# A decode-attention kernel re-cut into key quarters of all 16 heads, with its K turned on VectorE and one softmax for all

## Chip, cores, metric

One core of one Trainium2 chip. The metric is the device time of one execution in microseconds (us). A time is the median of several runs, or one run where that is said; the span of the profiled execution is some 2 us shorter than its run's time. Each run on record carries a state: "slow" when it is over 1.5% above the fastest of its kernel, "unknown" when it is single.

## The reference, cut to what matters

One decode step for a batch of 2: a layer norm of `x`, an attention over a sliding window of a K and V cache, and a gate from a small ReLU network. All inputs are bfloat16.

```python
# B, D = 2, 448;  Hq, Hkv, Sk, Dh = 16, 8, 8192, 256;  W = 2048 (the last 2048 keys)
q = (xn @ wq).reshape(B, 1, Hq, Dh)                    # wq: 448 x 4096
k, v = k_cache[:, :, Sk - W:], v_cache[:, :, Sk - W:]  # [2, 8, 2048, 256], two q heads share one
o = softmax(q k^T / 16) v
s = o.reshape(B, 1, 4096) @ wo                         # wo: 4096 x 448
g = silu(relu(xn @ w1) @ w2)                           # w1: 448 x 1792, w2: 1792 x 448
out = x + s * g
```

What must be read is 44.1 MB: 16.8 MB of K, 16.8 MB of V, and 10.5 MB of weights. "16 heads" below means the 2 x 8 pairs of batch and KV head. In the caches, the same key of two neighbouring heads lies 8192 x 256 x 2 bytes = 4 MiB apart.

## The kernel before

K and V come in four units of 4 MiB. A unit is four heads of one batch with all 2048 keys. Each SBUF partition gets one piece of 32 KiB (64 keys). The order of the source is "row of 64 keys outside, head inside":

```python
def kv_src(u, cache):
    b, v = divmod(u, 2)
    return cache[b, 4 * v:4 * v + 4, SK - W:SK, :].rearrange("h (r t) d -> r h (t d)", t=NT)  # NT = 64
# as built: source [step 32 KiB, 32] [step 4 MiB, 4] [32 KiB] -> 128 partitions of 32 KiB
```

PE (TensorE, the matrix engine) turns each K piece (as fp32 pairs of bf16), and VectorE (DVE) and ScalarE (ACT) evict it, that is, copy it out of PSUM:

```python
o = pr.op(PE, lambda e, n=n, lo=lo: e.matmul(bank_f[:, n * 128:(n + 1) * 128],
    lhsT=src_f[:, lo:lo + 128], rhs=ident_f[:, :], start=True, stop=True, is_transpose=True), deps)
...                                                     # cut
if i not in ON_ACT:
    evac[n_th] = pr.op(DVE, lambda e: e.tensor_copy(dst[:, :], bank[:, :]), deps)
else:
    evac[n_th] = pr.op(ACTE, lambda e: e.activation(dst[:, :], bank[:, :], ACT.Copy), deps)
```

Every unit has its own softmax chain (maximum, transposed maximum, shift, exp, transposed weights), and PV (weights times V) of a unit runs beside the scores of the next. The tail multiplies the attention output with `wo`, 32 row blocks of four matmuls each, none column-tiled, while the last pieces of `wo` land. All loads go through one queue, issued by SyncE (SP) in program order.

## Time and profile before

| | before |
|---|---|
| time, median of the first 3 runs | 112.46 us (112.26 to 113.44) |
| span of the profiled run | 110.4 us |
| read from HBM | 44.11 MB |
| PE, DVE, ACT busy | 71%, 45%, 33% of the span |

From the page of the profile of the kernel before: busy time and share of the span by engine, then the rate of the DMA in 40 equal slices of the span.

```profile
span 110.4 us, 1966 instructions
PE 78.2 (71%) x862; PEld 54.9 (50%) x867; DVE 49.4 (45%) x114; ACT 35.9 (33%) x44; POOL 2.3 (2%) x12
...
DMA  3989989998999899999999999999999999999930
GB/s 63 508 380 451 499 356 423 491 439 380 433 487 404 380 411 416 406 495 415 478 427 386 427 487 404 398 451 451 404 415 463 395 436 412 387 418 414 395 134 1
```

The same as a table of stretches. The columns are: the stretch in us, its length, the busy time (and instructions) of each engine, the granted clock of PE (1.00 is full), the DMA share (mean busy share of the 16 engines) and the rate.

```profile
core 0: us, PE busy (x) PEld busy (x) DVE busy (x) ACT busy (x) POOL busy (x), PEclk, DMA share, GB/s
20.00:30.00 10.00, 8.69 (x100) 6.54 (x103) 5.85 (x12) 4.99 (x6) 0.00 (x0) 1.00 1.02 438
...
40.00:50.00 10.00, 8.26 (x87) 5.08 (x87) 5.68 (x13) 3.88 (x5) 0.00 (x0) 1.00 1.03 430
...
80.00:90.00 10.00, 10.00 (x90) 8.12 (x88) 5.96 (x10) 6.77 (x7) 0.00 (x0) 0.88 0.98 418
...
105.00:107.00 2.00, 1.92 (x40) 1.75 (x38) 0.00 (x0) 0.00 (x0) 0.00 (x0) 1.00 0.43 167
```

The DMA share is near 1 from 2 to 105 us at about 425 GB/s, so the loads bound this kernel. No engine is busy all the time.

The groups of work that the change removes:

```profile
L301 PE MATMUL tb<-ident_f,kbuf 128*128 128x128 f32 x256 | 35.7, 300 | 10.9 <-DMA kbuf<-in_A_k_cache_dram 10.9
...
L311 ACT ACTIVATE kt<-tb 128x1024 bf16<-128x1024 bf16 x28 | 27.4, 1023 | 27.0 <-PE tb L301 27.0
L309 DVE COPY kt<-tb 128x1024 bf16<-128x1024 bf16 x36 | 24.7, 689 | 23.5 <-PE tb L301 23.4
```

The end of the chain of work that ended last (start us, length us, what):

```profile
79.70 27.09 DMA kbuf<-in_A_wo_dram
106.79 0.04 issue
106.83 1.36 PE obk L281 x24
...
108.22 0.27 DVE tmp L556
...
108.51 0.26 DVE out_sb L558
```

`wo` comes in six pieces. The one that lands at 106.79 us is the fifth: it releases the last 24 matmuls, and 3.6 us of work and store follow. The sixth and last is issued at 80.17 us and lands at 107.35, while they run; from there to the end it takes 3.1 us. Its line in the list of transfers (size, us from issue to landing):

```profile
kbuf<-in_A_wo_dram SPq DMA_DIRECT2D x1, 224.0 KB, 27.2
```

### The profile page before, as it was taken

How to read it: one execution, taken by the hardware profiler on the slowest of the kernel's cores; microseconds unless marked ns; L12 is line 12 of the kernel's file. 1: busy time of each engine (PE TensorE's matmuls, PEld its weight loads, DVE VectorE, ACT ScalarE, POOL GpSimd, SP SyncE). 2: the span in 40 equal slices, each digit the busy share in tenths (PEclk: the TensorE clock that was granted, in tenths of full speed). 3: DMA queues.
4: the chain of work that ended last, by engine and by line, in shares of the span. 5: the costliest groups of instructions: out<-in, count | busy, mean ns of one | idle time of the engine just before them, and what ended most of it. 6: DMA issues, size and time to landing. Idle time of an engine off the chain costs nothing.

```text
span 110.4 us, 1966 instructions
## 1 busy us (share of the span) xinstructions
PE 78.2 (71%) x862; PEld 54.9 (50%) x867; DVE 49.4 (45%) x114; ACT 35.9 (33%) x44; POOL 2.3 (2%) x12
## 2 busy tenths in 40 slices
PE   0010049997756999858589999856399985897991
PEld 0000049992322977322389876322397741335891
DVE  2292005485154666463401975463157655454001
ACT  4930004694002568402000948202046771200000
POOL 6200000000000000000000000000000000000000
PEclk9999999999999999999959999999859999999999
DMA  3989989998999899999999999999999999999930
GB/s 63 508 380 451 499 356 423 491 439 380 433 487 404 380 411 416 406 495 415 478 427 386 427 487 404 398 451 451 404 415 463 395 436 412 387 418 414 395 134 1
DMA packets 2907, 44.22 MB, mean 400 GB/s; under 512 B 338, under 2 KB 468, under 8 KB 1364
## 3 DMA queue, kind: packets, MB, share of 16 engines
q1 hardware_dynamic: 2864, 44.11, 94.2%
q8 instruction: 6, 0.10, 0.4%
q10 hardware_dynamic: 36, 0.01, 0.0%
q14 instruction: 1, 0.01, 0.0%
HBM read 44.11 MB, written 0.00 MB: 399 GB/s over the span
## 4 chain that ended last, share of the span: by engine, by line
PE 40%; DMA 37%; DVE 14%; SPq 3%; ACT 2%; issue 2%
DMA kbuf<-in_A_wo_dram 25%; PE tb L301 20%; DMA kbuf<-in_A_k_cache_dram 13%; PE sbk L281 6%; PE obk L281 4%; PE tb L281 4%; SPq L36 3%; DVE kt L309 2%; PE mbk L281 2%; DVE s_sb L351 2%; ACT e_sb L355 2%; DVE rm L334 2%; PE mbk L360 1%; DVE mrow L342 1%; PE mbk L339 1%
## 5 line engine op out<-in xcount | busy, mean ns | idle before, releaser
L301 PE MATMUL tb<-ident_f,kbuf 128*128 128x128 f32 x256 | 35.7, 300 | 10.9 <-DMA kbuf<-in_A_k_cache_dram 10.9
L301 PEld LDWEIGHTS tb<-ident_f,kbuf 128*128 128x128 f32 x256 | 31.9, 156 | 15.3 <-DMA kbuf<-in_A_k_cache_dram 11.0
L311 ACT ACTIVATE kt<-tb 128x1024 bf16<-128x1024 bf16 x28 | 27.4, 1023 | 27.0 <-PE tb L301 27.0
L309 DVE COPY kt<-tb 128x1024 bf16<-128x1024 bf16 x36 | 24.7, 689 | 23.5 <-PE tb L301 23.4
L281 PE MATMUL sbk<-kt,qz 128*32 128x512 bf16 x128 | 11.1, 393 | 1.6 <-DVE kt L309 1.1
L355 ACT ACTIVATE e_sb<-s_sb 128x512 bf16<-128x512 f32 x4 | 2.5, 629 | 21.4 <-DVE s_sb L351 21.4
L281 PE MATMUL obk<-vbuf,pt 128*16 128x512 bf16 x96 | 7.4, 379 | 0.0
L281 PE MATMUL obk<-kbuf,at_z 128*8 128x112 bf16 x128 | 7.0, 213 | 0.5 <-DMA kbuf<-in_A_wo_dram 0.3
L281 PEld LDWEIGHTS obk<-kbuf,at_z 128*8 128x8 bf16 x128 | 6.3, 87 | 1.0 <-DMA kbuf<-in_A_wo_dram 0.9
L281 PEld LDWEIGHTS sbk<-kt,qz 128*32 128x32 bf16 x128 | 2.7, 94 | 5.5 <-DVE kt L309 2.1
L281 PE MATMUL mbk<-ident,xg 2*128 2x2 bf16 x7 | 0.3, 163 | 6.6 <-DVE xg L246 6.6
L281 PE MATMUL tb<-qz,ident 128*128 128x512 bf16 x15 | 4.6, 382 | 0.3 <-issue 0.3
L334 DVE TENSOR_REDUCE rm<-sbk 128x4 f32<-128x512 f32 x4 | 2.8, 691 | 4.3 <-PE sbk L281 4.3
L281 PE MATMUL tb<-wf,h_z 128*8 128x112 bf16 x56 | 4.2, 258 | 0.4 <-DVE h_z L460 0.4
L281 PEld LDWEIGHTS tb<-wf,h_z 128*8 128x8 bf16 x56 | 4.1, 109 | 0.5 <-issue 0.5
L365 DVE COPY pt<-mbk 128x512 bf16<-128x512 bf16 x4 | 1.7, 424 | 5.0 <-PE mbk L360 5.0
L281 PEld LDWEIGHTS mbk<-ident,xg 2*128 2x128 bf16 x7 | 0.3, 101 | 6.6 <-DVE xg L246 6.6
L474 ACT ACTIVATE ea<-tb 8x112 f32<-8x112 f32 x1 | 0.3, 254 | 9.0 <-PE tb L281 9.0
L281 PE MATMUL mbk<-one_f,mall 1*128 1x1 f32 x8 | 1.5, 256 | 2.3 <-DVE mall L346 2.3
L339 PE MATMUL mbk<-ident_f,rm 128*1 128x128 f32 x4 | 1.1, 270 | 2.9 <-DVE rm L337 2.9
L351 DVE SCALAR_TENSOR_TENSOR s_sb<-sbk,bias,low 128x512 f32<-128x512 f32 x4 | 3.0, 751 | 0.1
L281 PEld LDWEIGHTS obk<-vbuf,pt 128*16 128x16 bf16 x96 | 2.1, 87 | 1.9
(77 smaller groups left out, 46.6 us busy)
## 6 DMA issues: line engine op xcount, KB each, us to landing
kbuf<-in_A_k_cache_dram SPq DMA_DIRECT2D x4, 4096.0 KB, 31.8
vbuf<-in_A_v_cache_dram SPq DMA_DIRECT2D x3, 4096.0 KB, 39.1
wf<-in_B_w_dram SPq DMA_DIRECT2D x2, 1568.0 KB, 43.8
vbuf<-in_A_v_cache_dram SPq DMA_DIRECT2D x1, 3072.0 KB, 19.6
vbuf<-in_A_wq_dram SPq DMA_DIRECT2D x1, 2560.0 KB, 19.7
kbuf<-in_A_wo_dram SPq DMA_DIRECT2D x2, 896.0 KB, 23.9
vbuf<-in_A_wq_dram SPq DMA_DIRECT2D x1, 1024.0 KB, 4.9
vbuf<-in_A_v_cache_dram SPq DMA_DIRECT2D x1, 1024.0 KB, 21.5
```

The lines of the kernel that those rows point to most:

```text
L36: o = _Op(eng, lambda e: e.dma_start(dst, src), [d for d in deps if d is not None], True)
L281: return lambda e: e.matmul(out_ap, lhsT=lhsT, rhs=rhs, start=start, stop=stop, skip_group_check=True, **kw)
L301: o = pr.op(PE, lambda e, n=n, lo=lo: e.matmul(bank_f[:, n * 128:(n + 1) * 128], lhsT=src_f[:, lo:lo + 128], rhs=ident_f[:, :], start=True ...
L309: evac[n_th] = pr.op(DVE, lambda e: e.tensor_copy(dst[:, :], bank[:, :]), deps)
L311: evac[n_th] = pr.op(ACTE, lambda e: e.activation(dst[:, :], bank[:, :], ACT.Copy), deps)
L334: v = pr.op(DVE, lambda e: e.tensor_reduce(out=rm4[:, :], in_=view(sbk, 0, [[1, 4], [4, 128]]), axis=AX.X, op=ALU.max), [st["S", u]])
L339: m = st["rmT", u] = pr.op(PE, lambda e: e.matmul(mbk_ap(0, 128, 1), lhsT=rm[:, :], rhs=ident_f[:, :], start=True, stop=True, is_transpose ...
L342: v = pr.op(DVE, lambda e: e.tensor_reduce(out=mrow[0:1, :], in_=view(mbk, 0, [[1, 8], [8, 16]], n=1), axis=AX.X, op=ALU.max, negate=True) ...
L351: v = st["shift", u] = pr.op(DVE, lambda e: e.scalar_tensor_tensor(out=s_sb[:, :], in0=sbk[:, :], scalar=bias[:, 0:1], in1=low[:, :], op0= ...
L355: a = st["exp", u] = pr.op(ACTE, lambda e: e.activation(e_sb[:, :], s_sb[:, :], ACT.Exp, accum_out=ssum[:, 0:1]), [v, st.get(("Pt", u - 1) ...
L360: o = pr.op(PE, lambda e, j=j: e.matmul(mb16[:, 512 + 128 * j:640 + 128 * j], lhsT=e_sb[:, 128 * j:128 * j + 128], rhs=ident[:, :], start= ...
L365: v = st["pt", u] = pr.op(DVE, lambda e: e.tensor_copy(view(pt[u % 2], 0, [[256, 2], [16, 16], [8, 2], [1, 8]]), view(mb16, 512, [[256, 2] ...
```

## The change

The intent: take 256 PE transposes and 64 evictions out, do one softmax for everything instead of four, and shorten the tail by column tiling. A unit is now a quarter of the keys (512) of all 16 heads, so that every row of scores belongs to one head; all K comes first, then all V. The core of the diff (cut; the setup of masks and selectors is left out):

```diff
         def kv_src(u, cache):
-            b, v = divmod(u, 2)
-            return cache[b, 4 * v:4 * v + 4, SK - W:SK, :].rearrange("h (r t) d -> r h (t d)", t=NT)
+            lo = SK - W + u * NT * NR                                     # NR = 8
+            return cache[:, :, lo:lo + NT * NR, :].rearrange("b h (r t) d -> (b h) r (t d)", t=NT)
...
         def do_T(u, i):                                                   # now do_T(u, blk)
-            ... 4 PE transposes into a PSUM bank, then a copy on DVE or ACT
+            st["T", u] = st["kt", u, blk] = pr.op(DVE, lambda e: e.transpose(
+                view(dst, 32 * NT * blk, [[1, 32 * NT]]), view(src, 32 * blk, [[DH // 2, NT], [1, 32]])),
+                [d_k[u], st.get(("S", u - 1, blk))])
...
-        def softmax(u, fill=()):                                          # once per unit
+        st["bias"] = pr.op(DVE, ... rm over all four units ...)           # once
+        def do_exp(u): / def do_spread(u): / def do_pt(u):                # exp, turn, spread, mask
...
+                o = pr.op(PE, mm(obk[64 * i:64 * i + 64, :], pt[u][:, 32 * t:32 * t + 64], ...,
+                                 u == 0 and t < 4, u == NU - 1 and t >= NT - 4, tile_position=(0, 64 * i)), deps)
...
-        for j in range(2 * NWO):                                          # 32 blocks, 4 matmuls each
+        for j in range(TILED):                                            # 24 blocks, one column-tiled matmul each
+            m_t = pr.op(PE, mm(tbk[32 * i:32 * i + B, 0:D], ..., tile_position=(0, 32 * i)), deps)
+        v_f = pr.op(DVE, lambda e: e.tensor_copy(wo_f[:, :], tbk[:, 0:D]), [m_t])
+        ... 8 blocks of 4 untiled matmuls, and 4 fp32 matmuls that fold the four column tiles in
```

As built, the source of a unit became [step 4 MiB, 16] [step 32 KiB, 8] [32 KiB]: its slowest dimension (the outermost one) went from 32 to 16.

## The prediction

> **What bounds the kernel now.** The inputs' traffic. The page's DMA section shows 44.11 MB read in a span of 110.4 us. In the table of stretches the DMA share is 0.96 to 1.04 in every stretch from 2 to 105 us, at 403 to 446 GB/s; summed, about 425 GB/s.[...] PE is busy 71%, DVE 45%, ACT 33% of the span. In the chain of waits the last wo piece lands at 106.8 us; then come 24 matmuls (1.36 us), two DVE operations (0.27 and 0.26) and the store: 3.6 us of tail.
>
> **What the change removes, none of it bounding.** 256 PE transposes (35.7 us busy), 64 evictions of kt (27.4 us ACT, 24.7 DVE), and three of four softmax chains (about 4 us each, from the row maximum to pt). Bytes stay the same.
>
> **What it adds.** 16 DVE transposes of 2048 fp32 columns. Estimate: a 512-column DVE operation from PSUM[...] takes 0.69 us here, of which some 0.16 is fixed (the tiniest operations' time), so 2048 columns take 2.2 to 2.3 us, 9.7 us for a unit with its maximum; a K unit arrives every 4.19 MB / 425 GB/s = 9.9 us. DVE just keeps pace. pt costs 16 tensor_tensor of about 0.7 us, 11 us, once.
>
> **Critical path (estimate: arrival = 2 us + bytes / 425 GB/s + 1 us).** wq 11.6, K0 to K3 21.5, 31.4, 41.2, 51.1, w1 and w2 58.7, V0 to V2 68.5, 78.4, 88.3, V3 98.1, wo 106.8 us. The queue must never run dry. K3 is issued after unit 0's transposes, about 32 (needed by 41); V0 about 42 (needed by 59), V1 51 (by 69), V2 61 (by 78), V3 after PV of unit 0, about 78 (by 88). All have 9 us or more to spare. Softmax and all pt, 62 to 80 us, hide behind V0 and V1. The last PV ends about 99.5, the attention output is spread by 101.5, when the first wo piece lands, and 24 column-tiled matmuls keep up with wo. The tail has 8 to 16 untiled matmuls at 57 ns, four fp32 fold matmuls (0.2 us each, if the last pieces land together) and the same DVE and store: 3.0 to 4.3 us against 3.6. So nearly all the work removed is off the path, and the time hardly moves.
>
> **Predicted:** 111.8 us, 109.8 to 115.0 (8 in 10). Faster by over 2%: 0.13; within 2%: 0.65; slower by over 2%: 0.22.
>
> **What would show it right.** DMA share near 1.0 at 420 to 430 GB/s from 2 to 105 us; the transposes at 2.2 to 2.3 us; PE and ACT busy far lower; the last wo piece landing at 106 to 107.5 us and still leading the chain of waits.
>
> **What would make it wrong.** (1) The rate. A unit now reads 16 heads, which lie 4 MiB apart[...].[...] If it holds, K and V alone cost tens of us more: look for a lower GB/s at a DMA share of 1. A slightly better rate could give 2 us. (2) A transpose of 3 us or more: DVE falls behind, V3 is issued after 88 us and the queue runs dry. (3) PE slow after idle waits in the last 10 us, lengthening the tail.

The sum: 106.8 us for the last landing and 3.0 to 4.3 for the tail make a span of 109.8 to 111.1, and some 2 us lie between span and time; the forecast was 111.8. In risk (1), "it" is a loss of rate for rows 4 MiB apart, which no trace had shown.

## The result

| | before | after |
|---|---|---|
| time, median | 112.36 us (4 runs) | 197.38 us (4 runs, 195.4 to 198.9) |
| span of the profiled run | 110.4 us | 193.6 us |
| read from HBM, mean rate over the span | 44.11 MB, 399 GB/s | 44.11 MB, 228 GB/s |
| PE, DVE, ACT busy | 71%, 45%, 33% | 35%, 33%, 5% |

The ratio is 1.747 (95% interval 1.729 to 1.766). Ratios are the mean time of one kernel's fast runs over that of the other's of the same rounds, so not quite the ratio of the medians quoted. One of the four runs after, 198.9 us, is slow.

The page of the kernel after:

```profile
span 193.6 us, 1150 instructions
PE 67.4 (35%) x488; PEld 28.5 (15%) x488; DVE 63.3 (33%) x79; ACT 9.4 (5%) x20; POOL 4.3 (2%) x13
...
PEclk9999955555555555555555585596558555795888
DMA  7999999999999899998999999999999999989960
GB/s 255 409 311 217 217 217 217 210 217 196 217 196 217 176 227 196 217 210 209 409 359 210 210 200 217 203 217 210 217 203 217 203 206 203 227 193 229 396 269 4
```

Here is the whole result. The DMA engines are as busy as before, at half the rate. The rate comes near 400 GB/s in three places only: at the start (`wq`), in the middle (`w1`, `w2`) and at the end (`wo`). Where K and V alone move, it is 176 to 229. The table of stretches of the kernel after:

```profile
core 0: us, PE busy (x) PEld busy (x) DVE busy (x) ACT busy (x) POOL busy (x), PEclk, DMA share, GB/s
20.00:40.00 20.00, 2.12 (x20) 0.57 (x18) 7.66 (x7) 0.00 (x0) 0.00 (x0) 0.58 1.00 210
40.00:60.00 20.00, 5.17 (x48) 0.53 (x40) 10.89 (x7) 0.00 (x0) 0.00 (x0) 0.50 1.00 210
...
140.00:160.00 20.00, 6.21 (x32) 2.58 (x32) 0.00 (x0) 0.00 (x0) 0.00 (x0) 0.59 1.00 211
...
180.00:185.00 5.00, 3.39 (x43) 1.21 (x39) 1.28 (x3) 0.75 (x2) 0.00 (x0) 0.97 0.99 410
```

From 140 to 160 us DVE and ACT do nothing and the rate is still 211, so it is not DVE's new work that slows the loads. The sum closes: 33.55 MB at 210 GB/s is 160 us, 10.55 MB at 400 is 26 us, together 186 us; the last piece of `wo` lands at 188.4.

The groups that replace those shown of before, and the line of the chain of waits:

```profile
DMA buf<-in_A_k_cache_dram 42%; DMA buf<-in_A_v_cache_dram 24%; DVE kt L286 9%; PE sbk L246 6%; PE obk L246 6%; PE pbk L246 1%; DVE e_t L328 1%; DVE rm L302 1%; PE mbk L246 1%; DVE o_sb L369 0%; ACT e_sb L325 0%; DVE q_t L318 0%; DVE q_n L316 0%; DVE qz L320 0%
...
L286 DVE STREAM_TRANSPOSE kt<-buf 128x2048 f32<-128x2048 f32 x16 | 36.0, 2286 | 53.7 <-DMA buf<-in_A_k_cache_dram 53.7
...
L246 PE MATMUL sbk<-kt,qz 128*8 128x512 bf16 x128 | 16.2, 610 | 65.9 <-DVE kt L286 48.1
...
L341 DVE TENSOR_TENSOR pt<-pbk,m 128x512 bf16<-128x512 f32 x16 | 9.8, 672 | 0.0
```

DVE's transposes take 2.29 us each and wait 53.7 us for K. PE's matmuls take longer than before (610 ns against 393 for the scores); the granted clock in those stretches is 0.5. That is not what costs the time: run e2 below has the same PE work, at a clock of 0.5 from 30 to 70 us, and takes 114 us. The tail of the kernel after, in order of time (start, length, engine, line, operation):

```profile
187.34 2.40 PE L246 MATMUL sbk<-kt,at_z 128*8 128x112 bf16 x24 [0.77 <-DMA kt<-in_A_wo_dram]
...
189.54 1.43 PE L246 MATMUL sbk<-wo_f,fold_z 128*8 128x112 f32 x8
...
190.80 0.56 PE L246 MATMUL sbk<-kt,at_z 128*8 128x112 bf16 x8
191.39 0.26 DVE L501 TENSOR_TENSOR tmp<-sbk,g_sb 8x112 f32<-8x112 f32 x1 [4.15 <-PE sbk L246]
191.69 0.26 DVE L503 TENSOR_TENSOR out_sb<-tmp,x_c 8x112 bf16<-8x112 f32 x1
```

The piece of `wo` that releases the 24 matmuls is here the fourth of six. From its landing (187.30) to the end it takes 6.3 us, against 3.6 before. From the landing of the very last piece (188.43, against 107.35 before) it takes 5.2 us against 3.1.

The trace also records size and duration of every DMA packet. A piece of 32 KiB of K or V took 1.22 us in the mean before (27 GB/s per DMA engine) and 2.48 us after (13 GB/s); the 28 KiB pieces of `wq` in the kernel after took 1.06 us in the median. So it is K's and V's packets that are slow, all 896 of this size. Packets of the weights that run beside them are slow too: those of `w1` and `w2` (12.25 KiB) took 0.82 us in the mean while K or V packets were in flight and 0.48 otherwise; in e2 below, with fast K and V, they took 0.47 beside them.

### The profile page after: what moved, and what is told of

Its sections match the earlier page's. It is cut to its first block, busy times and chain, and to the rows that moved or that the text cites. A ratio compares the mean times of both kernels' runs of the same rounds, so it can differ in the third digit from the quotient of the medians.

```text
span 193.6 us, 1150 instructions
## 1 busy us (share of the span) xinstructions
PE 67.4 (35%) x488; PEld 28.5 (15%) x488; DVE 63.3 (33%) x79; ACT 9.4 (5%) x20; POOL 4.3 (2%) x13
## 3 DMA queue, kind: packets, MB, share of 16 engines
q1 hardware_dynamic: 2720, 44.11, 96.2%
HBM read 44.11 MB, written 0.00 MB: 228 GB/s over the span
## 4 chain that ended last, share of the span: by engine, by line
DMA 66%; PE 14%; DVE 12%; another core or an unknown queue 5%; issue 1%; ACT 0%; SPq 0%
DMA buf<-in_A_k_cache_dram 42%; DMA buf<-in_A_v_cache_dram 24%; DVE kt L286 9%; PE sbk L246 6%; PE obk L246 6%; PE pbk L246 1%; DVE e_t L328 1%; DVE rm L302 1%; PE mbk L246 1%; DVE o_sb L369 0%; ACT e_sb L325 0%; DVE q_t L318 0%; DVE q_n L316 0%; DVE qz L320 0%
## 5 line engine op out<-in xcount | busy, mean ns | idle before, releaser
L286 DVE STREAM_TRANSPOSE kt<-buf 128x2048 f32<-128x2048 f32 x16 | 36.0, 2286 | 53.7 <-DMA buf<-in_A_k_cache_dram 53.7
L246 PE MATMUL sbk<-kt,qz 128*8 128x512 bf16 x128 | 16.2, 610 | 65.9 <-DVE kt L286 48.1
L246 PE MATMUL obk<-buf,pt 128*64 128x512 bf16 x128 | 24.5, 562 | 40.7 <-DMA buf<-in_A_v_cache_dram 40.7
L246 PEld LDWEIGHTS obk<-buf,pt 128*64 128x64 bf16 x128 | 9.8, 158 | 54.3 <-DMA buf<-in_A_v_cache_dram 42.6
L246 PE MATMUL pbk<-wf,xr_z 128*128 128x512 bf16 x28 | 8.0, 456 | 6.2 <-DMA wf<-in_A_wq_dram 6.2
L341 DVE TENSOR_TENSOR pt<-pbk,m 128x512 bf16<-128x512 f32 x16 | 9.8, 672 | 0.0
L246 PE MATMUL sbk<-kt,at_z 128*8 128x112 bf16 (+1 forms) x56 | 4.6, 308 | 2.5 <-DMA kt<-in_A_wo_dram 2.2
L246 PE MATMUL sbk<-wf,h_z 128*8 128x112 bf16 x56 | 5.1, 289 | 0.5 <-issue 0.5
L246 PEld LDWEIGHTS sbk<-wf,h_z 128*8 128x8 bf16 x56 | 5.0, 124 | 0.8 <-issue 0.8
L246 PE MATMUL sbk<-q_n,ident 128*128 128x512 bf16 x13 | 3.3, 381 | 0.0
```

The costliest lines, as they stand in the source:

```text
L246: return lambda e: e.matmul(out_ap, lhsT=lhsT, rhs=rhs, start=start, stop=stop, skip_group_check=True, **kw)
L286: st["T", u] = st["kt", u, blk] = pr.op(DVE, lambda e: e.transpose(view(dst, 32 * NT * blk, [[1, 32 * NT]]), view(src, 32 * blk, [[DH // 2 ...
L341: st["pt", u] = pr.op(DVE, lambda e, x=x: e.tensor_tensor(out=view(pt[u], 32 * x, [[128, 16], [8, 4], [1, 8]]), in0=view(pbk[u % 2], 128 * ...
```

## The experiments

The kernels read wrong keys, or put keys in wrong places, where that is said. The comparison with the reference sees little of the attention term; it says nothing about these kernels' correctness. That the times and rates do not depend on the values is my assumption; no run tests it alone. Beside a time stands that of the kernel before on the same chip. e2, e3 and e11 have several fast runs; all others are single looks (one run, state unknown) and are used only for differences far beyond the noise.

The first round had three theories. **A**: the heads lie 4 MiB apart and the engines read them side by side, so that they keep hitting the same part of the memory. This is the risk (1) of the prediction, a guess that no trace had shown. **B**: the new compute or the new order of the queue slows the loads. **C**: 16 heads spread over 64 MiB are slow in whatever order.

### e1: the new source alone, in the kernel before

```diff
-            b, v = divmod(u, 2)
-            return cache[b, 4 * v:4 * v + 4, SK - W:SK, :].rearrange("h (r t) d -> r h (t d)", t=NT)
+            lo = SK - W + u * NT * 8
+            return cache[:, :, lo:lo + NT * 8, :].rearrange("b h (r t) d -> (b h) r (t d)", t=NT)
```

> The kernel before, with only the source of its K and V loads replaced by that of the kernel after: 16 heads, 4 MiB apart, 8 rows of 32 KiB each (the numbers it computes are wrong on purpose). Theory A (heads 4 MiB apart[...] are read slowly): K and V drop to about 210 GB/s, the time rises from 112.4 to about 190 to 195 us, as after. Rival B (the new compute, DVE's transposes, the slower PE or the order of the queue slow the loads): time stays within 2% of 112.4.

Measured: 195.13 us (before 112.56), packets of 32 KiB 2.49 us in the mean. The source line alone does all of it. B is dead.

### e2: the old source alone, in the kernel after

```diff
-            lo = SK - W + u * NT * NR
-            return cache[:, :, lo:lo + NT * NR, :].rearrange("b h (r t) d -> (b h) r (t d)", t=NT)
+            b, v = divmod(u, 2)
+            return cache[b, 4 * v:4 * v + 4, SK - W:SK, :].rearrange("h (r t) d -> r h (t d)", t=NT)
```

> The kernel after, with only the source of its K and V loads replaced by that of the kernel before (4 heads of one batch[...]; wrong numbers on purpose). Theory A: about 420 GB/s in every stretch, 110 to 114 us (my prediction's 111.8 without its rate error). Rival B: stays above 180 us.

Measured: 113.99 us (before 112.56), ratio 1.0116 (1.0075 to 1.0157), packets 1.22 us. Everything else in the change together is worth plus 1.2%, slightly the wrong way. Two stretches of it, and then its tail in order of time:

```profile
40.00:50.00 10.00, 4.67 (x40) 0.42 (x32) 10.00 (x6) 0.00 (x0) 0.00 (x0) 0.50 0.99 423
...
107.00:109.00 2.00, 2.00 (x20) 1.83 (x19) 0.00 (x0) 0.00 (x0) 0.00 (x0) 0.50 0.04 8
```

```profile
105.39 0.62 DVE L485 COPY wo_f<-sbk 128x448 f32<-128x448 f32 x1 [3.56 <-PE sbk L246]
...
106.08 2.40 PE L246 MATMUL sbk<-kt,at_z 128*8 128x112 bf16 x24 [0.75 <-DMA kt<-in_A_wo_dram]
...
108.28 1.35 PE L246 MATMUL sbk<-wo_f,fold_z 128*8 128x112 f32 x8
...
109.47 0.56 PE L246 MATMUL sbk<-kt,at_z 128*8 128x112 bf16 x8
```

The last two pieces of `wo`, issued at 80.83 and 81.30 us, in its list of transfers:

```profile
kt<-in_A_wo_dram SPq DMA_DIRECT2D x2, 224.0 KB, 25.8
```

So the loads end at 107.15 us, 0.2 us earlier than in the kernel before (107.35). The 24 matmuls start at 106.08, when the fourth of six pieces has landed, but at a granted clock of 0.50 they take 100 ns each, where before had 24 at 57 ns. When the last piece lands, 12 of them have started; the rest, the fold and 8 more follow. From the last landing to the end it takes 5.1 us against 3.1, and 2.0 more less 0.2 is the whole difference of the two spans, 112.3 against 110.4.

### e3: 4 KiB off the step between heads

```diff
-            return cache[:, :, lo:lo + NT * NR, :].rearrange("b h (r t) d -> (b h) r (t d)", t=NT)
+            return bass.AP(cache.tensor, cache.offset + lo * DH,
+                           [[SK * DH - 8 * DH, B * HKV], [NT * DH, NR], [1, NT * DH]])
```

> The kernel after, with one number of its K and V sources changed: the step from head to head is 4 MiB minus 4 KiB (8 keys earlier for each further head; wrong keys on purpose). It is still 16 heads over 64 MiB[...]. Theory A (the same address modulo 4 MiB at the same moment): back to about 420 GB/s and 110 to 114 us. Rival C (16 heads spread over 64 MiB, however they are aligned): stays near 195 us.

Measured: 196.08 us (before 112.56), ratio 1.741 (1.734 to 1.749), packets 2.50 us. The alignment at 4 MiB is not what halves the rate. Theory A, my favourite, fails here.

### e4: the same 16 heads, the rows outside

```diff
-        def kv_src(u, cache):
-            lo = SK - W + u * NT * NR
-            return cache[:, :, lo:lo + NT * NR, :].rearrange("b h (r t) d -> (b h) r (t d)", t=NT)
+        def kv_src(u, cache, t0=0, t1=NT):
+            lo = SK - W + u * NT * NR + t0 // 2
+            return bass.AP(cache.tensor, cache.offset + lo * DH,
+                           [[32 * DH, 16], [2 * SK * DH, 8], [SK * DH, 2], [1, (t1 - t0) // 2 * DH]])
```

As built, 16 blocks of 32 keys (16 KiB) lie outside and the 16 heads inside. The idea was that engines working side by side would then read the same head, 16 KiB apart; which engine takes which block is not in the trace. (Cut from the diff: V's calls hand over their range of keys.)

> The kernel after, with the same 16 heads and the same bytes in each unit, but rows outermost[...] (wrong numbers on purpose). Theory A (what counts is what the engines read at the same time): about 420 GB/s and 110 to 115 us. Rival C (16 heads in one unit): stays near 195 us.

Measured: 196.52 us (before 112.56); its packets of 16 KiB took 1.25 us, again 13 GB/s per engine. Theory A fails a second time. After these four runs only C was left of the three, and one thing that I had not counted as a theory: all slow sources have a slowest dimension of 16, all fast ones 32 or 128 (K and V in before and e2, 1.22 us a packet of 32 KiB; the weights, 1.06 us a packet of 28 KiB of `wq`).

**Theory D.** The cause lies on the destination side, in how the engines share out the partitions that a transfer with slowest dimension 16 writes; C puts it on the source side. My expectations for e5 to e10 came from a picture of which engine writes which partitions at the same moment. By it, partitions 0 to 63 and 64 to 127 should be slow and 32 to 95 fast. No trace shows which engine writes which partition; what the runs can test is which partitions are fast. For a slow transfer I expected about the rate of the kernel after, which had 210 to 217 GB/s in its stretches of 20 us with K and V alone. D has a gap: it does not say why 32 outer elements are fast.

### e5: a compact source with slowest dimension 16

I first wrote the 32 rows of the kernel before as 16 x 2; the built program merged them back into 32, so that nothing would have changed. The run made groups that can't be merged (wrong keys):

```diff
-            return cache[b, 4 * v:4 * v + 4, SK - W:SK, :].rearrange("h (r t) d -> r h (t d)", t=NT)
+            return bass.AP(cache.tensor, cache.offset + (b * HKV + 4 * v) * SK * DH,
+                           [[8 * (NT + 1) * DH, 16], [NT * DH, 8], [1, NT * DH]])
```

> My theory A has fallen (e3, e4). New theory D: what halves the rate is how the 16 engines share out the destination.[...] This run: the kernel before, each unit read from 16 groups of 8 rows of 32 KiB that lie almost end to end (4 MiB in all, groups 260 KiB apart; wrong keys on purpose). Theory D: K and V at 210 to 218 GB/s, 190 to 197 us. Rival C (heads spread over 64 MiB, in whatever order): compact memory is fast, 112 to 114 us.

Measured: 196.41 us (before 113.75), packets 2.50 us. A source of 4 MiB in one place is as slow as 16 heads over 64 MiB (197.38 us, 2.48 us a packet).

### e6: 16 heads with slowest dimension 32

```diff
-            lo = SK - W + u * NT * NR
-            return cache[:, :, lo:lo + NT * NR, :].rearrange("b h (r t) d -> (b h) r (t d)", t=NT)
+            lo = SK - W + u * NT * NR // 2
+            return bass.AP(cache.tensor, cache.offset + (lo - SK // 2) * DH,
+                           [[SK * DH // 2, 32], [NT * DH, 4], [1, NT * DH]])
```

> The kernel after, each unit still spread over all heads and 62 MiB of the cache, but as 32 groups of 4 rows at a step of 2 MiB (slowest dimension 32 instead of 16; wrong keys on purpose). Theory D: fast, 420 GB/s and 113 to 115 us as e2. Rival C: stays near 195 us. Theory A in its first form (multiples of 2 or 4 MiB are bad) : well above 150 us.

Measured: 114.46 us (before 113.75), packets 1.22 us. A stretch of it while K moves:

```profile
20.00:40.00 20.00, 6.83 (x57) 1.10 (x58) 18.30 (x13) 0.00 (x0) 0.00 (x0) 0.69 0.98 421
```

Reading all heads over 62 MiB is fast if the slowest dimension is 32. C is dead. D was put down as predicting both e5 and e6, e6 with the gap named above. Besides, "a slowest dimension of 16 is slow, for whatever reason" would have predicted them too, so the next runs keep the 16 and move the destination.

### e7 and e8: 16 everywhere, other partitions

Each load of a unit is cut: in e7 into partitions 0 to 63 and 64 to 127, in e8 into 32 to 95, 0 to 31 and 96 to 127 (wrong layout).

```diff
+        PARTS = ((0, 0, 4), (64, 4, 4))                    # e7: first partition, first row, rows per head
+        PARTS = ((32, 0, 4), (0, 4, 2), (96, 6, 2))        # e8
-            d_k[u] = pr.dma(SP, buf[K_BUF[u]][:, :], kv_src(u, A_k_cache), [dep])
+            d_k[u] = [pr.dma(SP, buf[K_BUF[u]][p:p + 16 * n, :], kv_src(u, A_k_cache)[:, r:r + n, :], [dep])
+                      for p, r, n in PARTS]               # and V in the same way
```

> The kernel after, each load of a unit cut in two, slowest dimension 16 in both: 16 heads x 4 rows to partitions 0 to 63, 16 heads x 4 rows to partitions 64 to 127 (wrong layout on purpose). Control for e8. Theory D:[...]193 to 198 us.

Measured: 195.77 us (before 113.75), packets 2.49 us, not one of the 896 under 1.3 us.

> As e7, but cut as 16 heads x 4 rows to partitions 32 to 95, then 16 heads x 2 rows to 0 to 31 and to 96 to 127; still slowest dimension 16 everywhere, and one transfer more per unit. Theory D:[...]about 150 to 158 us in all, and packets of 32 KiB take 1.2 us in one half, 2.4 in the other. Any theory of the source side or of the dimension 16 alone: as e7, 193 us or more.

Measured: 178.48 us (before 113.75). The gain has the right sign, and 213 of 896 packets took under 1.3 us, in six bursts of 3 to 6 us. But half of them should have, and the time should have been 150 to 158. (An estimate from rates measured here comes near it: half of K and V at the 425 GB/s of the kernel before and half at the 210 of the kernel after is 119 us in place of 160, so about 157 in all.) In between, transfers to the middle and to the outer partitions are in flight together (K's take 29.9 and 37.1 us from issue to landing in the median), and my estimate had let the engines change over in step; that this is the whole shortfall was not shown.

### e9 and e10: one half only

To take the mixture away, these two load only 16 heads x 4 rows of each unit; the rest of the buffers is zeroed once by ACT.

```diff
+        PARTS = ((32, 0, 4),)                              # e9:  partitions 32 to 95
+        PARTS = ((0, 0, 4),)                               # e10: partitions 0 to 63
+        rest = [[pr.op(ACTE, lambda e, t=t, p=p, n=n: e.memzero(t[p:p + n, :])) for p, n in ((0, 32), (96, 32))][-1]
+                for t in buf]                              # e10: ((64, 32), (96, 32))
```

> The kernel after, but of each unit only half is loaded: 16 heads x 4 rows, to partitions 32 to 95 (the other partitions of the buffers are zeroed once by ACT; wrong numbers on purpose). The source pattern and the slowest dimension 16 are the same as in e10. Theory D[...]: nearly all 896/2 packets of 32 KiB take 1.2 us, K and V come at 400 GB/s or more whenever the queue is full. Any theory of the source side or of the dimension 16 alone: 2.3 to 2.6 us, as e10. The total is not bound by DMA here if D holds; I expect 85 to 105 us.

> As e9 with one change: the half goes to partitions 0 to 63[...]. Theory D: packets of 32 KiB take 2.4 to 2.6 us, K and V come at 210 to 218 GB/s, 105 to 115 us in all. A theory under which e8's gain came from something else than the choice of partitions: as e9.

Measured, with a stretch of each in which K moves (e9, then e10):

```profile
18.00:26.00 8.00, 1.79 (x9) 0.59 (x7) 4.28 (x2) 7.98 (x2) 0.00 (x0) 0.76 0.97 377
```

```profile
18.00:26.00 8.00, 2.69 (x13) 1.01 (x11) 3.29 (x2) 7.98 (x2) 0.00 (x0) 0.83 1.08 221
```

| packets of 32 KiB (448 each) | mean | 10%, median, 90% | under 1.3 us |
|---|---|---|---|
| e9, partitions 32 to 95 | 1.44 us | 1.21, 1.30, 1.96 | 223 |
| e10, partitions 0 to 63 | 2.53 us | 2.51, 2.55, 2.58 | 0 |

The source addresses, the slowest dimension 16, the number of partitions and the transfers are the same; only the first partition differs, 32 instead of 0. That decides for the destination (1.44 us a packet against 2.53, 391 GB/s against 241 from 10 to 24 us). The totals were 110.42 us for e9 (I expected 85 to 105; the zeroing on ACT, 42 us, and DVE behind it were on its path) and 116.48 us for e10 (expected 105 to 115). These totals say little, the packets what is asked.

Still, "nearly all at 1.2 us" did not come true for e9.

### e12: e9 with 4 KiB off the step between heads

The edit is that of e3, in e9. A stretch of it while K moves (e9 had 391 GB/s in the same stretch, e10 241):

```profile
10.00:24.00 14.00, 8.17 (x28) 3.12 (x28) 2.62 (x2) 13.96 (x3) 0.00 (x0) 0.95 1.01 432
```

> e9 with the step from head to head 4 MiB minus 4 KiB (wrong keys on purpose), as e3 had it. In e9 only half of the 32 KiB packets took the 1.21 us of a free engine; their mean was 1.44 us, not the 1.22 of e2 and e6. If that rest is the alignment of the heads in memory (theory A as a small second effect), the mean falls to 1.22 us here. If it is not, it stays at 1.4 to 1.5 us and its cause stays open. The total is not bound by DMA: 107 to 111 us either way.

Measured: 108.13 us; 366 of 448 packets under 1.3 us, mean 1.32 us, which lies between the two expectations. In the first long run of K, from 9 to 25 us, where the queue is full, the means of 4 us each are 1.34 to 1.38 us in e9 and 1.21 to 1.23 in e12. So theory A may be there as a small second effect, about 10%, visible only where the packets are fast (e3, with the same edit, had 2.50 us against 2.48 in the kernel after). These are single runs on different chips, though on 171 and 192 packets. Most of the slow packets left in both come at the start of later transfers, near 34, 60 and 70 us, after the queue had stood still: there the first 16 packets take 1.9 to 2.2 us in the mean. The first 16 packets of `wq` are slow in the same way, though they go to all 128 partitions (1.6 to 1.9 us, the rest 1.06 to 1.07, in the kernel after, e2, e6 and e9 to e12). So this goes with the start of a transfer and not with the choice of partitions; its cause stays open.

### e11: keeping PE awake in the tail of e2

```diff
         for j in range(TILED):
+            if d_wo.get(j) and j:
+                idle_work(4)
...
+            if j == TILED:
+                idle_work(4)
```

> e2 (114.0 us, 1.2% over the kernel before at the same DMA rate) with 4 idle matmuls put before each of the wo pieces at j = 12, 20, 24 and with them before the untiled part, so that PE does not fall to half clock while it waits. Theory: e2's extra comes from a tail of 4 us of matmuls at half clock (24 untiled in 2.4 us, 8 fp32 fold passes in 1.35, 8 untiled in 0.56): at full clock the tail falls by 1.2 to 1.8 us, to 112.2 to 112.8 us, level with the kernel before. If the idle matmuls only delay the real ones: 114 us or more.

Measured: 114.05 us (before 112.52), ratio 1.0116 (1.0059 to 1.0172); no gain over e2. In the profiled run the granted clock was 1.00 from 100 us on and the same three groups of matmuls took 1.34, 0.93 and 0.56 us instead of 2.40, 1.35 and 0.56. But the first of them began at 106.79 instead of 106.08, behind the last idle matmuls, although their piece had landed at 106.23. So the clock was the reason for the long groups, and the filling gave back a part of what it won. The profiled run, at 113.33, was also the fastest of the six; why the other five show no gain at all is not shown, since none of them has a trace. No run points to a version that beats the kernel before, and none was made.

## Why the prediction was wrong

- **What bounds the kernel: right.** DMA bound it before, and still does.
- **The step that failed** is the arrival estimate of the critical path, "arrival = 2 us + bytes / 425 GB/s + 1 us", in its 425 GB/s. "Bytes stay the same" held (44.11 MB in both), but I carried the rate of the old loads over to new loads with another access pattern. K and V moved at 210 GB/s (packets of 2.48 us instead of 1.22): 160 us for their 33.55 MB instead of 79, which adds about 80 us. The base of 425 was well measured, but for sources of 32 or 128 outer elements.
- **Risk (1) named the symptom, not the cause.** "look for a lower GB/s at a DMA share of 1" is just what came, and I gave slower 0.22. But I blamed heads 4 MiB apart. e3 and e4 refute that as the main cause: with other steps and another order the rate stayed halved. e5 and e6 show that the place in memory does not matter (2.50 us a packet from 4 MiB in one place, 1.22 from all heads over 62 MiB), and e9 against e10 that the partitions written do (1.44 against 2.53). The pitch may be worth about 10% (1.34 to 1.38 us in e9 against 1.21 to 1.23 in e12, one run each). A range that ended at 115 would have needed a reason to trust the rate, and I had none.
- **What is shown and what is not.** Shown: the cause lies in how a transfer with slowest dimension 16 meets the partitions (packets of 1.44 us to partitions 32 to 95 in e9, of 2.53 us to 0 to 63 in e10). Not shown: how the engines share out the partitions. The trace doesn't record which engine writes which partition. My picture of it expected e5, e7 and e10 as they came, and the direction of e8 and e9; it overstated the gain of e8, and it does not say why 32 outer elements are fast.
- **The compute terms: right.** Transposes 2.29 us (predicted 2.2 to 2.3), pt operations 0.67 us (about 0.7). With the old source (e2) the last PV ended at 99.7 us (predicted 99.5) and the last piece of `wo` landed at 107.15 (predicted 106.8).
- **The tail: mis-sized.** I put 3.0 to 4.3 us after the last landing; it was 5.1 in e2 and 5.2 after. I counted 8 to 16 untiled matmuls at 57 ns behind it. PE, at half clock, was still at the 24 of the pieces before (100 ns each, 12 not yet started in e2), and the fold (1.35 us) and 8 more came after them. This is risk (3), and with it the change at the full rate is 114.0 us, not 111.8. That 114.0 lies inside the predicted range is no success of the forecast: it is the time with the old source.
- **"Nearly all the work removed is off the path": right.** In e2, at an equal rate of the loads, PE is busy for 59.8 us instead of 78.2 and ACT for 9.4 instead of 35.9, and the time does not fall at all. (The halved share of PE in the kernel after is mostly the longer span.)

## What to carry to other kernels

When a change touches the access pattern of loads that bound the kernel, predict the rate anew instead of carrying it over: write down the built shape of source and destination, and time the packets of that shape in a run, with the partitions that it will write (2.48 us a packet of 32 KiB here against 1.22; by partitions alone, 2.53 in e10 against 1.44 in e9). In the profile here, a DMA share of 1 with half the GB/s (210 against 425) meant that each packet took twice as long, not that more bytes moved (44.11 MB in both); which loads are slow (here K and V) and the duration of one packet led to the cause. For K and V, an outer dimension of 32 elements over all 128 partitions was fast in every run here (1.22 us a packet in before, e2 and e6), one of 16 in one transfer over all 128 slow in every run (2.48 to 2.50 us in after, e1, e3 and e5).
